# One decode step of attention with a small dense layer: per-head results transposed on TensorE, finished on VectorE and mixed one piece apart, with the last values in four pieces

## The chip, the cores and the metric

The kernel runs on one core of one Trainium2 chip. The metric is the device time of one execution in microseconds (us); the number given for a kernel is the median of its runs. The profile comes from one separate execution, in which the hardware profiler records every instruction and every DMA packet.

## What is computed

The step takes two tokens (batch 2, one position each, width 448), a layer norm of them, and adds three things: the tokens themselves, attention over the last 4096 keys of a cache of 32768, and a dense layer with a mish activation (1792 wide). Cut to what matters:

```python
xn = _layernorm(x)
q  = (xn @ wq)                      # 16 heads of 256, 2 per key/value head
k, v = the last 4096 keys and values of each of the 8 key/value heads
p  = softmax(q k^T * 256**-0.5)
o  = p @ v
out = x + o.reshape(B, 1, 4096) @ wo + (mish(xn @ w1 + b1) @ w2)
```

Everything is bfloat16 in memory, and sums are kept in fp32. The bulk of the data is the cache: for each of 8 key/value heads 4 MiB of keys and 4 MiB of values, in all 64 MiB; the weights bring the total that is read to 77.67 MB.

## The kernel before

The 4096 keys of both batches are laid over 128 partitions, 64 keys in each (`T = 64`), and cut into four pieces of 16 (`TH`, `NH`). The main loop (`for i in range(Hkv + 1)`, L589 on) has one turn for each key/value head `i`, and an inner loop over its four pieces, numbered `s = 4 i + piece`.

For each piece:

- `turn(s+1)` (L404): VectorE transposes the next piece of keys in 32x32 blocks, `kt<-k`.
- `scores(s)` (L416): eight matmuls on TensorE, `sc<-kt,qdiag`, then two exponentials on ScalarE (L430), which also sum.
- `turn_p(s-1)` (L442): VectorE transposes the exponentials of the piece before, `pT<-p`. After the last piece of a head it forms the sums (L449, L451).

For each head, one head later:

- `values(i-1)` (L477): 32 matmuls `o<-v,pT`, with 8 rows of output: two positions at once (`NP = 2`), times batch and head. Only where the position in the row and the half of the output belong together is the result of use. The denominator is one fp32 matmul (L458, two records) and a reciprocal `rec` on VectorE (L462). ScalarE copies the output to SBUF, `o_sb` (L486).
- `values_fixed` (L554): the form that the last two heads (6 and 7, `NFIX = 2`) use instead: 128 matmuls with the values as the stationary operand, so that the result comes out already transposed; `scale_o` (L498) then divides.

Two heads later, after piece 0 of head `i`, `close(i-2)` runs `finish` and `mix`:

- `finish` (L516, L526, L532, L539), heads 0 to 5 only: TensorE multiplies `o_sb` by columns of an identity, 8 calls in fp32, which sum the two positions in PSUM as they transpose; then VectorE multiplies by `rec`, multiplies by `own` (which head a partition belongs to) and adds the two heads, giving `oTm`.
- `mix` (L220, for the last head L237): four matmuls of width 448 by `wo`, accumulated in one PSUM bank `psE`. For head 7 the output is split over four column groups (`psA`), into which `carry` (L249, L237) has brought the sum so far.

At the end `psA` is cast to `res` (L627) and written out (L628).

Transfers: all large loads are issued by SP in program order, keys of head i+1, then values of head i, then `wo` of head i (L373, L390, L398). A load waits for its buffer: keys and values have two buffers each. The keys of head 7 come in two pieces, its values in three (cut at 32, 56 and 64 of the 64 positions), its `wo` in two.

The order on each engine is the order in which the program is written: `issue_in_order` ties every instruction to the one before it on its engine. So where `finish` stands in the program decides which instructions of VectorE and TensorE it is queued behind and which wait behind it.

Of the kernel before, what the change touches and what calls it, by code (L numbers as in the profile page):

```python
# [34 lines left out]
def kernel(  # L35
# [13 lines left out]
    nc = tc.nc  # L49
# [48 lines left out]

    x_bf = consts.tile([Bsz, D], BF16)
    nc.scalar.dma_start(out=x_bf[:, :], in_=A_x.flatten_outer_dims())  # L100
    b1_sb = consts.tile([1, F], BF16)
    nc.scalar.dma_start(out=b1_sb[:, :], in_=B_b1.rearrange("(o f) -> o f", o=1))


    def v_tile():
# [97 lines left out]
    for par in range(2):  # L203
        for x in range(NX):
# [5 lines left out]
                scalar2=None,  # L210
                op0=ALU.mult,
            )
    ones = consts.tile([1, Bsz], BF16)
    nc.vector.memset(ones[:], 1.0)


    psE = ps_a.tile([Bsz, D], FP32, name="psE")

# [77 lines left out]
                )  # L296


    act_bf = consts.tile([P, NF, NX, Bsz], BF16)
    dense = {}  # L300

# [13 lines left out]

    def dense_in():
        w1_v = dense.pop("w1").rearrange("p s (q c) -> p s c q", c=NF)
        b1_v = b1_sb[:].rearrange("o (x q c) -> o x c q", x=NX, c=NF)
        hT_ps = ps_m.tile([P, NF, NX, Bsz], FP32, tag="m", name="hT_ps")
        for c in range(NF):  # L320
            for s in range(NS):
                nc.tensor.matmul(
                    hT_ps[:, c, :, :].rearrange("p x b -> p (x b)"),
                    lhsT=w1_v[:, s, c, :],
                    rhs=xs[:, s, :, :].rearrange("p x b -> p (x b)"),
                    start=(s == 0),
                    stop=False,
                    skip_group_check=True,
                )
            for x in range(NX):  # L330
                nc.tensor.matmul(
                    hT_ps[:, c, x, :],
                    lhsT=b1_v[:, x, c, :],
                    rhs=ones[:, :],
                    start=False,
                    stop=True,
                    skip_group_check=True,
                )
        shape = [P, NF, NX, Bsz]
        h_sb = consts.tile(shape, FP32, name="h_sb")  # L340
        nc.vector.tensor_copy(out=h_sb[:], in_=hT_ps[:])
        u_sb = consts.tile(shape, FP32, name="u_sb")
        nc.scalar.activation(out=u_sb[:], in_=h_sb[:], func=ACT.Exp)
        t_sb = consts.tile(shape, FP32, name="t_sb")
        nc.vector.scalar_tensor_tensor(
            out=t_sb[:], in0=u_sb[:], scalar=2.0, in1=u_sb[:], op0=ALU.add, op1=ALU.mult
        )
        den = consts.tile(shape, FP32, name="den_sb")
        nc.vector.tensor_scalar(
            out=den[:], in0=t_sb[:], scalar1=2.0, scalar2=None, op0=ALU.add  # L350
        )
        nc.vector.reciprocal(out=den[:], in_=den[:])
        nc.vector.tensor_tensor(out=t_sb[:], in0=t_sb[:], in1=den[:], op=ALU.mult)
        nc.vector.tensor_tensor(out=act_bf[:], in0=h_sb[:], in1=t_sb[:], op=ALU.mult)  # L354
# [24 lines left out]
    def load_v(i, cuts=(0, T)):  # L379
        t = v_tile()  # L380
        load_cache(t, A_v_cache, i, cuts)
        v_t[i] = t[:].rearrange("p (t d) -> p t d", t=T)
# [17 lines left out]
    def turn(s):  # L400
        kt = kt_pool.tile([P, TH * Dh], BF16, tag="kt", name="kt")
        i, half = divmod(s, NH)
        k = k_t[i] if half < NH - 1 else k_t.pop(i)
        nc.vector.transpose(  # L404
            out=kt[:].bitcast(FP32),
            in_=k[:, half * TH * Dh : (half + 1) * TH * Dh].bitcast(FP32),
        )
        kt_t[s] = kt
# [47 lines left out]
    def denominator(i):  # L456
        den = ps_m.tile([P, BR], FP32, tag="m", name="den")
        nc.tensor.matmul(  # L458
            den[:], lhsT=ones_f[:], rhs=state.pop(("sums", i))[:], start=True, stop=True
        )  # L460
        rec = small.tile([P, BR], FP32, tag="rec", name="rec")
        nc.vector.reciprocal(out=rec[:], in_=den[:])  # L462
        return rec
# [6 lines left out]
    def values(i):  # L470

        po = ps_o.tile([NR, NP * Dh], FP32, tag="o", name="o")
        v = v_t.pop(i)
        state["rec", i] = denominator(i)
        for u in range(T // NP):
            piece, uh = divmod(u, TH // NP)
            nc.tensor.matmul(  # L477
                po[:],
                lhsT=pT_t[i * NH + piece][:, uh * NP * Q : (uh + 1) * NP * Q : HS],
                rhs=v[:, u * NP : (u + 1) * NP, :].rearrange("p t d -> p (t d)"),  # L480
                start=(u == 0),
                stop=(u == T // NP - 1),
            )
        o_sb = small.tile([NR, NP, NJ, rep, PH], FP32, tag="o_sb", name="o_sb", bufs=1)
        for u in range(NP):
            nc.scalar.copy(  # L486
                out=o_sb[:, u, :, :, :],
                in_=po[:, u * Dh : (u + 1) * Dh]
                .rearrange("r (m j) -> r j m", j=NJ)
                .unsqueeze(2)  # L490
                .to_broadcast([NR, NJ, rep, PH]),
            )
        state["o", i] = o_sb
# [12 lines left out]
        )  # L506
        state["oT", i] = oT

    def finish(i):

        o_sb = state.pop(("o", i))
        pq = ps_q.tile([P, NJ * BR], FP32, tag="q", name="q")
        pqv = pq[:].rearrange("p (j r) -> p j r", j=NJ)
        for j in range(NJ):
            for u in range(NP):
                nc.tensor.matmul(  # L516
                    pqv[:, j, :],
                    lhsT=o_sb[:, u, j, :, :].rearrange("r h m -> r (h m)"),
                    rhs=ident_f[0:NR, u * BR : (u + 1) * BR],
                    start=(u == 0 and j == 0),  # L520
                    stop=(u == NP - 1),
                    skip_group_check=True,
                )
        rec = state.pop(("rec", i))
        o = small.tile([P, NJ, Bsz, rep], FP32, tag="osum", name="osum")
        nc.vector.tensor_tensor(  # L526
            out=o[:].rearrange("p j b h -> p j (b h)"),
            in0=pqv,
            in1=rec[:].unsqueeze(1).to_broadcast([P, NJ, BR]),
            op=ALU.mult,  # L530
        )
        nc.vector.tensor_tensor(  # L532
            out=o[:].rearrange("p j b h -> p j (b h)"),
            in0=o[:].rearrange("p j b h -> p j (b h)"),
            in1=own[:].rearrange("p b h -> p (b h)").unsqueeze(1).to_broadcast([P, NJ, BR]),
            op=ALU.mult,
        )
        oT = small.tile([P, NJ, Bsz], BF16, tag="oTm", name="oTm")
        nc.vector.tensor_tensor(  # L539
            out=oT[:], in0=o[:, :, :, 0], in1=o[:, :, :, 1], op=ALU.add  # L540
        )
        state["oT", i] = oT

    def values_fixed(i):
# [19 lines left out]
    def mix(kvh):  # L564
        oT = state.pop(("oT", kvh))
        w = wo_t.pop(kvh)
        put = add_last if kvh == Hkv - 1 else add
        if kvh < Hkv - NFIX:
            for j in range(NJ):
                add(oT[:, j, :], w[:].rearrange("p h (c d) -> p (h c) d", c=ND)[:, j, :])  # L570
            return
        for h in range(rep):
            for c in range(ND):
                put(
                    oT[:, c, h, :],
                    w[:, h, c * D : (c + 1) * D],
                    stop=(kvh >= Hkv - 2 and h == rep - 1 and c == ND - 1),
                )

    def close(i):  # L580
        if i < Hkv - NFIX:
            finish(i)
        mix(i)

    load_k(0)
    load_dense()
    project()
# [3 lines left out]
    for i in range(Hkv + 1):  # L591
        if i + 1 < Hkv:
            load_k(i + 1, (0, T) if i + 1 < Hkv - 1 else (0, T // 2, T))
        if i < Hkv:
            load_v(i, (0, T) if i < Hkv - 1 else (0, T // 2, 7 * T // 8, T))
            load_wo(i, parts=1 if i < Hkv - 1 else 2)
            for piece in range(NH):
                s = i * NH + piece
                if s + 1 < NSTEP:
                    turn(s + 1)  # L600
                scores(s)
                if s >= 1:
                    turn_p(s - 1)
                if s == NSTEP - 1:
                    turn_p(s)
                if piece == 0 and i > 1:
                    close(i - 2)
            if i + 2 < Hkv:
                build_q(i + 2)
        else:  # L610
            close(i - 2)
            carry()
        if i == 0:
            dense_in()
            dense_out()
        if i >= 1:
            if i - 1 < Hkv - NFIX:
                values(i - 1)
            else:
                values_fixed(i - 1)  # L620
        if i == Hkv:
            close(i - 1)

    res = consts.tile([Bsz, D], BF16)
    for n in range(NO):
# [34 lines left out]
```

The softmax here doesn't subtract the row's maximum and nothing guards it: scores larger than these inputs give would overflow.

## Time and profile before

| what | value |
|---|---|
| median of 11 runs | 192.11 us (190.89 to 193.04) |
| the profiled execution's own time | 191.89 us |
| its span, first to last instruction | 190.0 us |
| TensorE busy, share of the span | 154.3 us, 81% |
| VectorE busy | 108.7 us, 57% |
| ScalarE busy | 45.4 us, 24% |
| GpSimd busy | 16.4 us, 9% |
| moved by DMA | 77.81 MB, mean 409 GB/s over the span |
| granted TensorE clock, mean | 0.898 of full |

In the profile a group reads "line, engine, operation, out<-in, shape, count, busy time, mean of one". Fp32 matmuls leave two records for each call. "PEld" is the load of the stationary operand, which runs beside the matmuls. A wait is put down to the instruction that ended it. The chain of work is followed back from the last instruction, at each step to what released it.

### The profile page before, as it was taken

To read this page: it belongs to the slowest core of one execution; us is meant where nothing else is said; L and a number is where in the kernel's file an instruction comes from. 1 tells how busy PE (TensorE), PEld (TensorE's weight loads), DVE (VectorE), ACT (ScalarE), POOL (GpSimd) and SP (SyncE) were. 2 spreads that over 40 slices of the span, in tenths; PEclk is the share of its full clock that TensorE was granted. 3 is DMA by queue.
4 is the path that set the end of the run, shared out by engine and by line. 5 is a ranking of instruction groups with operands and counts; after the bars stand their busy time and mean duration, and the time that the engine had idled before them with its cause. 6 is when DMAs were issued, how large, how long until landed. Compare 5 with 4: busy or idle time off the path is not lost.

```text
span 190.0 us, 2498 instructions
## 1 busy us (share of the span) xinstructions
PE 154.3 (81%) x981; PEld 75.0 (39%) x981; DVE 108.7 (57%) x144; ACT 45.4 (24%) x148; POOL 16.4 (9%) x74
## 2 busy tenths in 40 slices
PE   0397099905989989998999889779895889989983
PEld 0133033902334344435343534253442534534762
DVE  6703697059572957097806990399209957576211
ACT  3003115200152223222332242222403151404201
POOL 7000600300003000300030003000300000000000
PEclk9999759955899978999699999999999999979755
DMA  6999999999999999999999899999999999999950
GB/s 218 429 458 434 394 480 415 407 438 421 441 434 435 443 424 441 422 441 419 450 424 436 382 473 434 407 441 424 434 441 441 396 439 448 438 406 421 417 224 0
DMA packets 4884, 77.81 MB, mean 409 GB/s; under 512 B 517, under 2 KB 1033, under 8 KB 2186
## 3 DMA queue, kind: packets, MB, share of 16 engines
q1 hardware_dynamic: 4868, 77.66, 95.8%
q8 instruction: 7, 0.11, 0.2%
q14 instruction: 3, 0.02, 0.0%
q10 hardware_dynamic: 6, 0.01, 0.0%
HBM read 77.67 MB, written 0.00 MB: 409 GB/s over the span
## 4 chain that ended last, share of the span: by engine, by line
DMA 49%; PE 31%; DVE 16%; SPq 1%; issue 1%; ACT 1%; ACTq 0%; DVEq 0%
DMA k<-in_A_k_cache_dram 49%; DVE kt L404 12%; PE sc L416 10%; PE o L477 7%; PE psE L220 4%; PE q L516 4%; PE q L554 4%; DVE pT L442 2%; PE psA L237 1%; ACT p L430 1%; PE den L458 0%; SPq L114 0%; DVE osum L532 0%; DVE osum L526 0%; DVE oTm L539 0%
## 5 line engine op out<-in xcount | busy, mean ns | idle before, releaser
L404 DVE STREAM_TRANSPOSE kt<-k 128x2048 f32<-128x2048 f32 x32 | 73.1, 2288 | 45.8 <-DMA k<-in_A_k_cache_dram 45.8
L416 PE MATMUL sc<-kt,qdiag 128*128 128x512 bf16 x256 | 65.0, 407 | 13.4 <-DVE kt L404 13.4
L430 ACT ACTIVATE p<-sc,off 128x256 bf16<-128x256 f32 x64 | 33.1, 544 | 71.5 <-PE sc L416 70.8
L416 PEld LDWEIGHTS <-qdiag 128*128 128x128 bf16 x256 | 24.6, 101 | 53.6 <-issue 18.6
L477 PE MATMUL o<-v,pT 128*8 128x512 bf16 x192 | 42.5, 379 | 0.0
L477 PEld LDWEIGHTS <-pT 128*8 128x8 bf16 x192 | 17.2, 92 | 22.4
L442 DVE STREAM_TRANSPOSE pT<-p 128x512 bf16<-128x512 bf16 x32 | 21.7, 678 | 6.4 <-ACT p L430 6.4
L289 POOL COPY qdiag<-qt 32x16 bf16<-32x16 bf16 x64 | 12.9, 248 | 120.5 <-PE sc L416 102.9
L486 ACT COPY o_sb<-o 8x512 f32<-8x512 f32 x12 | 6.3, 573 | 36.3 <-PE o L477 36.3
L516 PEld LDWEIGHTS q<-ident_f,o_sb 8*128 8x128 f32 x96 | 11.1, 186 | 2.5 <-issue 2.5
L430 ACT ACTIVATION_READ_ACCUMULATOR p<-sc,off 128x1 f32 x64 | 11.7, 183 | 0.0
L516 PE MATMUL q<-ident_f,o_sb 8*128 8x4 f32 x96 | 11.7, 249 | 0.0
L269 PE MATMUL q_ps<-v,xq 128*128 128x512 bf16 x28 | 9.1, 504 | 2.1 <-DVE xq L260 2.1
L220 PE MATMUL psE<-v,act_bf 128*2 128x448 bf16 x14 | 4.8, 528 | 6.4 <-DVE act_bf L354 6.4
L220 PE MATMUL psE<-wo,oTm 128*2 128x448 bf16 x24 | 6.4, 394 | 4.1 <-DVE oTm L539 4.1
L554 PEld LDWEIGHTS <-v 128*128 128x128 bf16 x256 | 7.3, 102 | 0.0
L554 PE MATMUL q<-pT,v 128*128 128x4 bf16 x256 | 7.1, 168 | 0.0
L269 PEld LDWEIGHTS <-xq 128*128 128x128 bf16 x28 | 3.4, 124 | 7.8 <-issue 3.8
L279 DVE CAST q_sb<-q_ps 128x512 bf16<-128x512 f32 x2 | 1.3, 686 | 8.6 <-PE q_ps L269 8.6
L220 PEld LDWEIGHTS <-act_bf 128*2 128x2 bf16 x14 | 1.5, 116 | 9.3 <-DVE act_bf L354 6.5
L190 PE MATMUL xnT_ps<-ident,xn_bf 2*128 2x2 bf16 x7 | 0.5, 166 | 5.7 <-DVE xn_bf L138 5.7
L526 DVE TENSOR_TENSOR osum<-q,rec 128x16 f32<-128x16 f32 x6 | 1.0, 174 | 6.7 <-PE q L516 6.7
(62 smaller groups left out, 49.0 us busy)
## 6 DMA issues: line engine op xcount, KB each, us to landing
k<-in_A_k_cache_dram SPq DMA_DIRECT2D x7, 4096.0 KB, 28.4
v<-in_A_v_cache_dram SPq DMA_DIRECT2D x7, 4096.0 KB, 27.6
k<-in_A_k_cache_dram SPq DMA_DIRECT2D x2, 2048.0 KB, 24.3
v<-in_B_w_dram SPq DMA_DIRECT2D x2, 1568.0 KB, 24.8
wo<-in_A_wo_dram SPq DMA_DIRECT2D x7, 448.0 KB, 28.6
v<-in_A_wq_dram SPq DMA_DIRECT2D x1, 2048.0 KB, 7.7
v<-in_A_v_cache_dram SPq DMA_DIRECT2D x1, 2048.0 KB, 15.0
v<-in_A_wq_dram SPq DMA_DIRECT2D x1, 1536.0 KB, 10.9
```

Of the source, the lines that this page charges most:

```text
L220: nc.tensor.matmul(psE[:], lhsT=lhsT, rhs=w, start=start, stop=stop, skip_group_check=True)
L237: nc.tensor.matmul(part(n), lhsT=lhsT, rhs=w[:, n * DO : (n + 1) * DO], start=start, stop=stop, tile_position=(0, n * Q), skip_group_check ...
L269: nc.tensor.matmul(ps[u][:], lhsT=xq[:, s, :, :].rearrange("p j k -> p (j k)"), rhs=wq_sb[:, s, u * N5 : (u + 1) * N5], start=(s == 0), st ...
L289: nc.gpsimd.tensor_copy(out=tv[rows, :, e, j * Q : (j + 1) * Q : HS].rearrange("p n (b h) -> p n b h", b=Bsz), in_=qv[rows, :, h0 : h0 + r ...
L404: nc.vector.transpose(out=kt[:].bitcast(FP32), in_=k[:, half * TH * Dh : (half + 1) * TH * Dh].bitcast(FP32),)
L416: nc.tensor.matmul(psc[:], lhsT=qdiag[i % NW][:, n * NE + e, :], rhs=ktv[:, n, e, :, :], start=(n == 0 and e == 0), stop=(n == NB - 1 and ...
L430: nc.scalar.activation(out=pv[:, b, :, :], in_=sv[:, b, :, :], func=ACT.Exp, scale=scale, bias=off[:, b : b + 1], accum_out=state["rs", i] ...
L442: nc.vector.transpose(out=pT[:], in_=p_t.pop(s)[:])
L477: nc.tensor.matmul(po[:], lhsT=pT_t[i * NH + piece][:, uh * NP * Q : (uh + 1) * NP * Q : HS], rhs=v[:, u * NP : (u + 1) * NP, :].rearrange ...
L486: nc.scalar.copy(out=o_sb[:, u, :, :, :], in_=po[:, u * Dh : (u + 1) * Dh] .rearrange("r (m j) -> r j m", j=NJ) .unsqueeze(2) .to_broadcas ...
L516: nc.tensor.matmul(pqv[:, j, :], lhsT=o_sb[:, u, j, :, :].rearrange("r h m -> r (h m)"), rhs=ident_f[0:NR, u * BR : (u + 1) * BR], start=( ...
L554: nc.tensor.matmul(po[:, c, :], lhsT=vv[:, t, c, :], rhs=pTv[:, th, 0:Q:HS], start=(t == 0 and c == 0), stop=(t == T - 1), skip_group_chec ...
```

## The change

- `finish` is split. `turn_o(i-2)` does the TensorE part where `close` stood, after piece 0; `finish(i-2)` does the VectorE part in piece 1, after that piece's `turn` and ahead of its `scores`; `mix(i-2)` comes at the end of piece 1. In the program's order TensorE now has scores, transpositions, scores, mix; and VectorE has one more `kt` transposition ahead of the finishing instructions.
- The eight fp32 matmuls of `finish` become eight fp32 transpositions with an 8-column identity each. They no longer sum the two positions; all 8 rows come out.
- VectorE then multiplies the two useful halves (two instructions of 128x16) and sums positions and heads with one reduction. The mask `own` is multiplied into `rec` once, in `values`, by one instruction of 128x4 (`recm`).
- The values of head 7 come in four pieces (cut at 32, 52, 60 and 64) in place of three.
- The bias of the dense layer is laid over two partitions and added by one matmul in place of two for each of seven groups (`half` in place of `ones`).

```diff
-    b1_sb = consts.tile([1, F], BF16)
-    nc.scalar.dma_start(out=b1_sb[:, :], in_=B_b1.rearrange("(o f) -> o f", o=1))
+    b1_sb = consts.tile([NX, HF], BF16)
+    nc.scalar.dma_start(out=b1_sb[:, :], in_=B_b1.rearrange("(x f) -> x f", x=NX))
...
-            for x in range(NX):
-                nc.tensor.matmul(
-                    hT_ps[:, c, x, :],
-                    lhsT=b1_v[:, x, c, :],
-                    rhs=ones[:, :],
...
+            nc.tensor.matmul(
+                hT_ps[:, c, :, :].rearrange("p x b -> p (x b)"),
+                lhsT=b1_v[:, c, :],
+                rhs=half[:].rearrange("o x b -> o (x b)"),
...
-        state["rec", i] = denominator(i)
+        rec = denominator(i)
+        state["rec", i] = small.tile([P, BR], FP32, tag="recm", name="recm")
+        nc.vector.tensor_tensor(
+            out=state["rec", i][:],
+            in0=rec[:],
+            in1=own[:].rearrange("p b h -> p (b h)"),
+            op=ALU.mult,
+        )
...
-    def finish(i):
+    def turn_o(i):
 
         o_sb = state.pop(("o", i))
-        pq = ps_q.tile([P, NJ * BR], FP32, tag="q", name="q")
-        pqv = pq[:].rearrange("p (j r) -> p j r", j=NJ)
+        pq = ps_q.tile([P, NJ * NP * NR], FP32, tag="q", name="q")
+        pqv = pq[:].rearrange("p (j u r) -> p j u r", j=NJ, u=NP)
         for j in range(NJ):
             for u in range(NP):
-                nc.tensor.matmul(
-                    pqv[:, j, :],
-                    lhsT=o_sb[:, u, j, :, :].rearrange("r h m -> r (h m)"),
-                    rhs=ident_f[0:NR, u * BR : (u + 1) * BR],
-                    start=(u == 0 and j == 0),
-                    stop=(u == NP - 1),
-                    skip_group_check=True,
+                nc.tensor.transpose(
+                    pqv[:, j, u, :],
+                    o_sb[:, u, j, :, :].rearrange("r h m -> r (h m)"),
+                    ident_f[0:NR, 0:NR],
                 )
+        state["pq", i] = pqv
+
+    def finish(i):
+        pqv = state.pop(("pq", i))
         rec = state.pop(("rec", i))
-        o = small.tile([P, NJ, Bsz, rep], FP32, tag="osum", name="osum")
...
+        o = small.tile([P, NJ, NP, BR], FP32, tag="osum", name="osum")
+        for u in range(NP):
+            nc.vector.tensor_tensor(
+                out=o[:, :, u, :],
+                in0=pqv[:, :, u, u * BR : (u + 1) * BR],
+                in1=rec[:].unsqueeze(1).to_broadcast([P, NJ, BR]),
+                op=ALU.mult,
+            )
         oT = small.tile([P, NJ, Bsz], BF16, tag="oTm", name="oTm")
-        nc.vector.tensor_tensor(
-            out=oT[:], in0=o[:, :, :, 0], in1=o[:, :, :, 1], op=ALU.add
-        )
+            nc.vector.tensor_reduce(
+                out=oT[:],
+                in_=o[:].rearrange("p j u (b h) -> p j b u h", b=Bsz),
+                axis=AXIS.XY,
+                op=ALU.add,
+            )
...
-            load_v(i, (0, T) if i < Hkv - 1 else (0, T // 2, 7 * T // 8, T))
+            load_v(i, (0, T) if i < Hkv - 1 else (0, T // 2, 13 * T // 16, 15 * T // 16, T))
...
                 if s + 1 < NSTEP:
                     turn(s + 1)
+                if piece == 1 and i > 1:
+                    finish(i - 2)
                 scores(s)
...
                 if piece == 0 and i > 1:
-                    close(i - 2)
+                    turn_o(i - 2)
+                if piece == 1 and i > 1:
+                    mix(i - 2)
             if i + 2 < Hkv:
                 build_q(i + 2)
         else:
-            close(i - 2)
+            mix(i - 2)
             carry()
...
         if i == Hkv:
-            close(i - 1)
+            mix(i - 1)
```

## Prediction

> **What bounds the kernel now.** I read the slices of the page first, then the DMA issues, then the chain of work over the last 35 us, and last the granted clock there.
>
> ```profile
> PEclk9999759955899978999699999999999999979755
> DMA  6999999999999999999999899999999999999950
> ...
> v<-in_A_v_cache_dram SPq DMA_DIRECT2D x7, 4096.0 KB, 27.6
> ...
> v<-in_A_v_cache_dram SPq DMA_DIRECT2D x1, 1536.0 KB, 18.1
> v<-in_A_v_cache_dram SPq DMA_DIRECT2D x1, 512.0 KB, 18.7
> wo<-in_A_wo_dram SPq DMA_DIRECT2D x2, 224.0 KB, 18.6
> ```
>
> The DMA engines are full from the first slices to slice 38 of 40. A 4 MiB load takes 27.6 us from issue to landing though its bytes alone need 4.19 MB / 0.43 MB per us = 9.8 us: some 18 us of older loads stand ahead of each at its issue. A buffer released a few microseconds later costs nothing, so before about 180 us an engine can neither gain nor lose time for the kernel. The last loads are issued at about 164.1, 164.7 and 166.0 us; with the landing times above, the values of head 7 are complete at 183.4 and the last half of `wo` at 184.6. The end of the span is 190.0, 5.4 us later. What lies in between is shown by the chain:
>
> ```profile
> 156.45 7.01 PE o L477 x32
> 163.46 1.85 PE sc L416 x8
> 165.30 1.89 PE q L516 x16
> ...
> 167.63 0.18 DVE oTm L539
> 167.81 0.04 issue
> 167.85 1.27 PE psE L220 x4
> 169.12 6.61 PE sc L416 x24
> 175.73 0.12 PE den L458 x2
> 175.85 3.43 PE q L554 x128
> ...
> 182.95 3.43 PE q L554 x128
> 186.38 0.02 issue
> 186.40 0.18 DVE oT L498
> 186.58 0.04 issue
> 186.62 0.65 PE psA L237 x16
> ```
>
> TensorE works without a DMA wait from 156.45 on and is late: when the last values land at 183.4 it has just begun the 128 matmuls of head 7 (end 186.37). So the end is set by TensorE's backlog, and the floor under it is the last load. In the backlog are the fp32 matmuls L516 (1.9 us) and a wait for `oTm` (167.17 to 167.85, 0.68 us).
>
> ```profile
> 167.00:168.00 1.00, 0.33 (x3) 0.17 (x3) 0.72 (x4) 0.00 (x0) 0.00 (x0) 1.00 0.91 393
> 168.00:169.00 1.00, 1.00 (x4) 0.17 (x2) 1.00 (x1) 0.00 (x0) 0.00 (x0) 0.64 1.14 492
> 169.00:170.00 1.00, 1.00 (x4) 0.39 (x4) 1.00 (x2) 0.00 (x0) 0.00 (x0) 0.50 1.14 492
> 171.00:172.00 1.00, 1.00 (x4) 0.39 (x3) 1.00 (x1) 0.00 (x0) 0.00 (x0) 0.65 0.81 321
> ```
>
> The third number from the end is the granted clock. Right after L516 and that wait it falls to half, from 168.3 to 171.65 us, and this slows the scores: 24 matmuls in 6.61 us, while 16 of the turn before took 3.66 (0.229 each, 5.5 for 24).
>
> [...] No run here shows an fp32 transposition yet. [...]
>
> **The change part by part**, on the profiled execution (own time 191.89, of which 190.0 span; 0.22 under the median 192.11).
>
> 1. Transpositions for matmuls. Now 16 records, 1.94 us for a head. Eight transpositions of one pass each at 0.112 are 8 x 0.112 + 0.14 (drain) = 1.04, a gain of 0.9. [...] I take 0.9. It counts once, at head 5's results (165.23); the other five groups lie under the DMA stream.
>
> 2. `finish` and `mix` a piece later. At the tail TensorE goes from the transpositions (end 166.3) straight to scores of piece 29, whose keys are turned at 163.2. VectorE turns piece 30 meanwhile (from 164.1 to 166.4; its keys landed earlier: 9.3 MB follow them in the stream, 184.2 - 9.3 / 0.43 = 162.6), finishes from 166.4 to 167.0, and `mix` on TensorE at about 168.1 finds `oTm` ready. The wait of 0.68 us goes. Next late is VectorE: `pT` (0.67) and piece 31 (2.3) end at 170.0; TensorE needs piece 31 at about 171, so nothing new waits.
>
> 3. In turns 2 to 6 of the loop VectorE starts from a late landing of keys, and there the same order adds a wait. In turn 6: piece 26 is turned at 148.5 to 150.8, `finish` follows to 151.5, and `mix` stands in TensorE's queue from about 149.6 (scores of 25 end) to 151.6. Queued behind are the scores of 26 (then 152.5 to 154.3). The scores of 27 need piece 27, turned at 152.0 to 154.3 as now: VectorE loses nothing, since its 0.20 us wait for L516 goes and `recm` comes. They begin at 154.4 as now (154.43). [...]
>
> 4. The half clock at 168.3. The low-activity stretch that called it (165.23 to 167.85, 2.6 us) shrinks to 1.0 us of transpositions. If the spell goes, its cost goes: 3.35 us at half speed, 1.65 us. Bounds 0 and 1.65.
>
> 5. VectorE: two products of 0.175 and one reduction (nearest row L539, 0.17; L449 on fewer outputs 0.12) for three instructions of 0.17; plus `recm` 6 x 0.17 after `rec`. At head 5 it stands ahead of piece 29 and moves its end from 163.18 to 163.35, which TensorE wants at 166.3: nothing.
>
> 6. Values in four pieces. SP issues one DMA more, 0.54 to 0.6 us, before `wo` of head 7; that is issued at 166.6 in place of 166.0, with 18 us of stream ahead: nothing. The last piece is 4 positions in place of 8: 8 matmuls after its landing in place of 16, at 0.028 us (3.55 / 128) a gain of 0.22, but only if TensorE is there first. Bounds 0 and 0.22, and up to 0.2 lost if smaller pieces slow the stream.
>
> 7. Bias: seven matmuls less at 34 to 38 us, about 0.13 each, where TensorE then idles 6.4 us for `act_bf`; `half` delays `xq` by 0.1 us at 8.5 us, under a stream 18 us ahead: nothing.
>
> Sum on the path. Points 1 and 2: 0.9 + 0.68 = 1.58. L554 of head 7 then ends at 186.37 - 1.58 = 184.8, just after the last load (184.6): span 188.4. With point 4 too, TensorE would be 3.2 us earlier, but the loads stop it: values 183.4, 8 matmuls and drain to 183.8, `oT` to 184.05, the second half of `mix` not before 184.6, ended at 185.0 in place of 187.2: gain 2.2, span 187.8. The phase of the clock is free, so I take 2.0: 191.89 - 2.0 = 189.9, and from the median 192.11 - 2.0 = 190.1 us.
>
> **The rivals.** A, the forecast: backlog gone, the end a little behind the last load; 190.1, by itself 189.4 to 191.0. B: an fp32 transposition is as slow as the matmul pair, and half clock comes all the same; only the wait goes, 192.11 - 0.7 = 191.4. [...] C: the stream ends later (five small loads at its end, or a slower transfer), which takes back the gain: 192.1. Against it: the same bytes behind the same backlog. [...]
>
> **How the numbers follow.** A 0.72, B 0.14, C 0.07, D 0.07. The likeliest is A. Some of A's upper end falls to "same". 0.5% is 0.96 us, about what a measurement of this kernel can tell from no change: faster 0.72, same 0.20, slower 0.08. The range runs from 189.2 (all of 2.2, a fast transposition, a stream at its best) to 191.7, which takes in B.
>
> **What would show it.** The transposition group at half the records and about 1 us for a head; no wait of TensorE for `oTm` at the tail, but one of about 2 us in each of turns 2 to 6; full clock from 165 to 175; L477 of head 5 ending at 163.5 still; the last DMA at 184 to 185; `psA` starting near 184.5 to 185. I am wrong if the L477 end moves, if the stream ends later, or if the records of the transpositions stay at sixteen.

## The result, and the profile after

The changed kernel takes 189.81 us (median of 12 runs, 189.50 to 190.28), the kernel before 191.79 us (median of 47 runs, 190.87 to 193.08). The ratio is 0.989, with a 95% interval from 0.987 to 0.992. The profiled execution took 189.74 us, its span 187.9 against 190.0. The runs of the changed kernel also lie closer together: 0.8 us from the lowest of 12 to the highest, against 2.2 us in 47. A ratio here and below compares runs within 1.5% of the fastest of their kernel; only the kernel with the repeated transpositions has longer ones, six of 22.

The slices of the page after, granted clock and DMA:

```profile
PEclk9999558955699999995799999985999999999855
DMA  6999899999999999999999999999999999999990
```

The stream is as it was, and full one slice further towards the end of a shorter span. The mean granted clock of the profiled execution is lower than before (0.870 against 0.898): there is more half clock in the middle (84.5 to 91.35 and 125.45 to 132.3 us), and it is gone from where it counted. The chain of waits of the changed kernel, from 155 us on (start, duration, what):

```profile
155.84 0.12 PE den L458 x2
155.96 7.02 PE o L484 x32
...
166.22 0.59 SPq L398
166.81 0.04 issue
166.85 17.76 DMA wo<-in_A_wo_dram
184.62 0.04 issue
184.66 0.46 PE psA L234 x8
185.12 0.23 ACT res L634
```

Before, TensorE and VectorE stood in every line of this chain from 156 us to the end of the last `mix`, but for gaps of 0.02 to 0.04 us. Now a transfer ends it: the second half of `wo` for head 7 lands at 184.62, eight matmuls follow, and the end. The landing itself has hardly moved (184.6 before). The time came out of the 2.7 us between that landing and the end of the last `mix`, of which 0.5 are left.

Where TensorE's lateness went is seen in the order of time, changed kernel, TensorE's own lines (start, duration, engine, line, operation; in brackets its idle time and what ended it):

```profile
162.90 1.91 PE L416 MATMUL sc<-kt,qdiag 128*128 128x512 bf16 x8
164.74 0.66 PE L523 MATMUL q<-ident_f,o_sb 8*128 8x8 f32 x8
165.33 1.91 PE L416 MATMUL sc<-kt,qdiag 128*128 128x512 bf16 x8
167.18 0.92 PE L217 MATMUL psE<-wo,oTm 128*2 128x448 bf16 x4
168.03 3.66 PE L416 MATMUL sc<-kt,qdiag 128*128 128x512 bf16 x16
172.32 3.56 PE L562 MATMUL q<-pT,v 128*128 128x4 bf16 x128 [0.52 <-DMA v<-in_A_v_cache_dram]
181.75 2.22 PE L562 MATMUL q<-pT,v 128*128 128x4 bf16 x64 [0.94 <-DMA v<-in_A_v_cache_dram]
```

The transpositions are eight records in 0.66 us where sixteen in 1.94 stood. `mix` starts with no wait for `oTm`. The last 16 score matmuls need 3.66 us, at full clock. From 172 us on TensorE waits for values twice, 0.52 and 0.94 us, and the last 64 matmuls take 2.22 us where the 64 before them took 1.85, so some 0.35 us more of waiting lie between their pieces: it is ahead of the loads. The granted clock (third number from the end), changed kernel, in the microseconds in which it was halved before:

```profile
167.00:168.00 1.00, 1.00 (x6) 0.25 (x4) 1.00 (x2) 0.72 (x3) 0.00 (x0) 1.00 0.76 328
168.00:169.00 1.00, 1.00 (x6) 0.49 (x6) 1.00 (x1) 0.36 (x2) 0.00 (x0) 1.00 1.06 459
169.00:170.00 1.00, 1.00 (x6) 0.39 (x5) 1.00 (x2) 0.02 (x1) 0.00 (x0) 1.00 1.14 492
171.00:172.00 1.00, 0.80 (x6) 0.47 (x3) 0.71 (x1) 0.34 (x3) 0.00 (x0) 1.00 0.84 333
```

### The profile page after: what moved, and what is told of

Same layout as the page of the kernel before. It is cut to its first block, busy times and chain, and to the rows that moved or that the text cites. A ratio compares the mean times of both kernels' runs of the same rounds, so it can differ in the third digit from the quotient of the medians.

```text
span 187.9 us, 2389 instructions
## 1 busy us (share of the span) xinstructions
PE 148.8 (79%) x926; PEld 67.4 (36%) x926; DVE 108.6 (58%) x150; ACT 45.3 (24%) x148; POOL 16.3 (9%) x74
## 4 chain that ended last, share of the span: by engine, by line
DMA 66%; DVE 20%; PE 8%; SPq 2%; ACT 1%; issue 1%; ACTq 0%; DVEq 0%
DMA k<-in_A_k_cache_dram 57%; DVE kt L404 16%; DMA wo<-in_A_wo_dram 9%; PE sc L416 4%; PE o L484 4%; DVE pT L442 3%; SPq L373 2%; ACT p L430 1%; PE psE L217 0%; SPq L114 0%; DVE sums L451 0%; SPq L398 0%; DVE oTm L544 0%; DVE recm L476 0%; PE psA L234 0%
## 5 line engine op out<-in xcount | busy, mean ns | idle before, releaser
L416 PE MATMUL sc<-kt,qdiag 128*128 128x512 bf16 x256 | 66.9, 413 | 16.2 <-DVE kt L404 15.9
L484 PE MATMUL o<-v,pT 128*8 128x512 bf16 x192 | 42.5, 379 | 0.0
L484 PEld LDWEIGHTS <-pT 128*8 128x8 bf16 x192 | 17.2, 92 | 22.4
L217 PE MATMUL psE<-v,act_bf 128*2 128x448 bf16 x14 | 5.4, 574 | 6.4 <-DVE act_bf L354 6.4
L266 PE MATMUL q_ps<-v,xq 128*128 128x512 bf16 x28 | 8.2, 465 | 2.1 <-DVE xq L257 2.1
L562 PE MATMUL q<-pT,v 128*128 128x4 bf16 x256 | 7.6, 169 | 1.5 <-DMA v<-in_A_v_cache_dram 1.5
L523 PEld LDWEIGHTS q<-ident_f,o_sb 8*128 8x128 f32 x48 | 4.1, 162 | 3.4 <-issue 3.4
L217 PEld LDWEIGHTS <-oTm 128*2 128x2 bf16 x24 | 1.7, 89 | 8.5 <-DVE oTm L544 6.2
L523 PE MATMUL q<-ident_f,o_sb 8*128 8x8 f32 x48 | 4.7, 220 | 0.0
```

Of the source, the lines that this page charges most:

```text
L217: nc.tensor.matmul(psE[:], lhsT=lhsT, rhs=w, start=start, stop=stop, skip_group_check=True)
L266: nc.tensor.matmul(ps[u][:], lhsT=xq[:, s, :, :].rearrange("p j k -> p (j k)"), rhs=wq_sb[:, s, u * N5 : (u + 1) * N5], start=(s == 0), st ...
L416: nc.tensor.matmul(psc[:], lhsT=qdiag[i % NW][:, n * NE + e, :], rhs=ktv[:, n, e, :, :], start=(n == 0 and e == 0), stop=(n == NB - 1 and ...
L484: nc.tensor.matmul(po[:], lhsT=pT_t[i * NH + piece][:, uh * NP * Q : (uh + 1) * NP * Q : HS], rhs=v[:, u * NP : (u + 1) * NP, :].rearrange ...
L523: nc.tensor.transpose(pqv[:, j, u, :], o_sb[:, u, j, :, :].rearrange("r h m -> r (h m)"), ident_f[0:NR, 0:NR],)
L562: nc.tensor.matmul(po[:, c, :], lhsT=vv[:, t, c, :], rhs=pTv[:, th, 0:Q:HS], start=(t == 0 and c == 0), stop=(t == T - 1), skip_group_chec ...
```

## The experiments

The theory (A): TensorE's backlog set the end, partly made of work and a wait, partly of a half-clock spell; the change removes more than it has to, and the last load is the new limit. The rivals: the transpositions alone carry it, the later place alone carries it, the smaller last piece carries it, or the clock plays no part. Each kernel was timed beside runs of the kernel before on the same chip, whose medians were 192.18 (first four), 191.87 (next four) and 192.21 us (last four). The changed kernel was not timed again beside them; differences from it are taken from its 189.81, which one version in each group that was expected to take the same time comes close to (189.58, 189.84 and 189.74).

### One part at a time

**Only the later place.** The kernel before, with the three calls set where the changed kernel has them; the fp32 matmuls and VectorE's instructions stay.

```diff
-    def finish(i):
+    def turn_o(i):
...
+        state["pq", i] = pqv
+
+    def finish(i):
+        pqv = state.pop(("pq", i))
         rec = state.pop(("rec", i))
...
+                if piece == 1 and i > 1:
+                    finish(i - 2)
                 scores(s)
...
-                    close(i - 2)
+                    turn_o(i - 2)
+                if piece == 1 and i > 1:
+                    mix(i - 2)
```

> The kernel before with only the order changed: the fp32 matmuls of finish stay, the finishing on VectorE and mix come one piece later. Theory A (the end was set by TensorE's backlog, the floor is the last load): at the tail the wait of 0.68 us for oTm goes and nothing else, unless the half-clock spell goes too; 191.1 with the spell, 189.8 without, so between 189.8 and 191.1 by its phase. Rival T (the cheaper transpositions carry the gain): 191.8, as before. Rival D (a slower middle): over 192.5, with the values of head 5 ending later than 163.5.

Measured: 189.79 us, ratio 0.990 (0.988 to 0.993). This is the whole gain, at the favourable end of what A allowed, although the sixteen records of L516 are still there. Its chain of waits:

```profile
156.12 7.02 PE o L477 x32
163.15 0.02 issue
163.16 0.54 SPq L373
163.71 0.05 issue
163.76 18.45 DMA v<-in_A_v_cache_dram
182.21 0.05 issue
182.25 1.88 PE q L558 x64
184.13 0.02 issue
184.16 0.18 DVE oT L498
```

Here, too, a load bounds the end: the middle one of the three loads of values (1536 KB) lands at 182.21, and the 64 matmuls that are left run through behind it. The clock is full from 48.2 to 177.9 us. Rival T falls.

**Only the transpositions.** The changed kernel with the old order and three pieces, so with VectorE's new instructions too. The new bias stays: by the author's account the old one, laid out on one partition, does not fit in SBUF beside the larger tiles of the sums; no run shows it.

```diff
-                if piece == 1 and i > 1:
-                    finish(i - 2)
...
                     turn_o(i - 2)
-                if piece == 1 and i > 1:
+                    finish(i - 2)
                     mix(i - 2)
...
-            load_v(i, (0, T) if i < Hkv - 1 else (0, T // 2, 13 * T // 16, 15 * T // 16, T))
+            load_v(i, (0, T) if i < Hkv - 1 else (0, T // 2, 7 * T // 8, T))
```

> The kernel before with only the fp32 transpositions, the sums on VectorE and the new bias, all in the old place after piece 0 (the old bias does not fit beside the larger tiles); values of head 7 in three pieces. Theory A: the 16 records of 1.94 us become 8 of 0.66, so TensorE is 1.28 us less late, the wait for oTm stays near 0.7, and the low-activity stretch is 1.3 us instead of 2.6, so the half clock should mostly go: 189.8 to 190.5. Rival M (the later place carries the gain): 191.8.

Measured: 189.97 us, ratio 0.991 (0.989 to 0.994). The wait for `oTm` at the tail is still there:

```profile
PE psE L217 <- DVE oTm L544: 0.6, 1, 0.6
```

The clock is full from 48.4 to 178.1 us. Rival M falls as well: either part alone is enough.

**Only the pieces and the bias.**

```diff
-            load_v(i, (0, T) if i < Hkv - 1 else (0, T // 2, 7 * T // 8, T))
+            load_v(i, (0, T) if i < Hkv - 1 else (0, T // 2, 13 * T // 16, 15 * T // 16, T))
```

(and the bias of two partitions, as in the change).

> The kernel before with only the four pieces of the last values and the bias in one matmul per group. Theory A: TensorE is behind the last load anyway, so nothing: 191.8. Rival P (the smaller last piece is what shortens the end): 190 or below. A third reading, that one more small load makes the stream longer: 192.0 or above.

Measured: 191.71 us, ratio 0.999 (0.997 to 1.001): nothing. Its chain ends as that of the kernel before does, to within 0.05 us (head 7's last matmuls end at 186.37), and half clock stands at 168.6 to 172.0 again.

**The change without the four pieces** (the same line, the other way round).

> The changed kernel with the last values in three pieces as before. Theory A: with TensorE ahead of the loads, 16 matmuls follow the last piece in place of 8, which is 0.22 us, but the last half of wo lands about 1 us after the values and hides it: 189.8. Rival P (the pieces matter once TensorE is ahead): 190.0 or more, and the second half of mix starts without a wait for wo.

Measured: 189.58 us, ratio 0.989 (0.987 to 0.992). With TensorE ahead, too, the fourth piece is worth nothing that can be seen: the matmuls of the values then end at 184.04, while `wo` lands about as late. One part of A's reason did not hold, that `wo` lands 1 us later and hides the 16 matmuls: `mix` ran through behind the values, and the profile names no wait for `wo`. The two are level, and the end is in the same place.

### The clock

**More work in the kernel before.** Where it idled just before the half clock, it does eight score matmuls a second time, with no reader.

```diff
     def close(i):
         if i < Hkv - NFIX:
             finish(i)
+        if i == Hkv - NFIX - 1:
+            filler((i + 2) * NH + 1)
         mix(i)
```

> The kernel before with more work: in the last turn that has a finish, the eight score matmuls of piece 29 are also done once more, between the fp32 matmuls and mix, into a tile that nobody reads. That is 1.73 us of busy TensorE, of which 0.68 lie where it waits for oTm anyway: 1.05 us more on the path. Clock theory (the low-activity stretch of the fp32 matmuls and the wait calls half clock at 168.3, which costs 1.65 us): the stretch is filled, full clock from 165 to 175, and the time goes down by some 0.6 us, 191.2, with 190.5 to 191.5 as its range. Rival (only the amount of work counts): 192.8 or above.

Measured: 191.47 us, ratio 0.998 (0.996 to 1.000). The kernel does about 1 us more on TensorE's path and takes 0.4 us less by the medians. The interval touches 1, so it is not slower, and "faster" is at the edge; the 192.8 of the rival is out. Two lines of its windows and its chain of waits show the cause:

```profile
168.00:169.00 1.00, 1.00 (x6) 0.33 (x5) 1.00 (x1) 0.00 (x0) 0.00 (x0) 1.00 1.21 524
170.00:171.00 1.00, 1.00 (x6) 0.48 (x5) 1.00 (x2) 0.00 (x0) 0.00 (x0) 1.00 0.67 279
```

```profile
165.27 1.87 PE q L516 x16
167.14 1.85 PE sc_more L585 x8
168.99 0.85 PE psE L220 x4
169.84 5.34 PE sc L416 x24
```

The 24 score matmuls take 5.34 us at full clock; they took 6.61 in the kernel before. `psE` takes 0.85 in place of 1.27. So 1.7 us of lost clock came back for 1.1 us of work. That the half clock merely fell elsewhere in this execution can be ruled out: the two earlier spells stand where they stood (69.4 to 72.8 and 89.9 to 93.3 us here, 69.3 to 72.7 and 89.8 to 93.2 before), and only the one behind the filled gap is missing.

**More tiny work in the changed kernel.** The eight transpositions of head 5 are done seven times.

```diff
-        for j in range(NJ):
+        for j in list(range(NJ)) * (7 if i == Hkv - NFIX - 1 else 1):
             for u in range(NP):
                 nc.tensor.transpose(
```

> The changed kernel with the eight transpositions of head 5 repeated six times more: 48 x 0.066 = 3.2 us more of TensorE work of low activity at the place where the fp32 matmuls stood. Nearly as much work as in the run with the score matmuls of two pieces twice. Clock theory: a stretch of 3.8 us of tiny instructions calls half clock for the scores after it, 1.65 us on top: 192.7 to 193.1. Rival (only the amount counts): 191.2 to 191.6.

Measured: 192.64 us, median of 22 runs that spread from 190.23 to 194.76; 192.53 without the six longest, and a ratio of 1.000 (0.998 to 1.003). That is just under the 192.7 to 193.1 of the clock theory, and 0.9 over the top of what the rival allowed. It is also 1.0 us more than the kernel below that adds 3.46 us of full-width work, for less added work (3.2 us at full clock). The profiled run (194.26) is one of the six. In it half clock lasts from 167.5 to 174.35, 6.85 us or twice the 3.35 of the kernel before, and begins inside the string: 39 of the 56 transpositions start in the 2.4 us before 167.5, the other 17 take 2.0 us, some 4.3 us in all. So 3.7 us were added there, of which some 0.5 us is half clock itself. The wide spread of the runs would fit a spell that varies in length and place, but no second run was profiled.

### How far TensorE is ahead

**Eight, then sixteen score matmuls more at the tail.**

```diff
-        for n in range(NB):
+        for n in list(range(NB)) * (2 if s in (NSTEP - 2,) else 1):
             for e in range(NE):
                 nc.tensor.matmul(
                     psc[:],
```

and `(NSTEP - 2, NSTEP - 1)` for sixteen.

> The changed kernel with the eight score matmuls of piece 30 done twice: 1.73 us more of busy TensorE at the tail. Theory A (TensorE is ahead of the loads; its waits for values are 0.52 and 0.94 us there): the reserve of about 1.5 us takes nearly all of it, 189.8 to 190.2. Rival (TensorE still sets the end): 191.5.

Measured: 189.84 us, ratio 0.988 (0.983 to 0.992): 1.73 us of work cost nothing.

> The changed kernel with the score matmuls of pieces 30 and 31 done twice: 3.46 us more. Theory A: beyond the reserve of about 1.5 us every microsecond counts, so 1.6 to 2.0 us more than the changed kernel, 191.4 to 191.8. If the reserve is larger than read: 190.5 or below. If TensorE sets the end all along: 193.2.

Measured: 191.52 us, ratio 0.997 (0.995 to 1.000): the second 1.73 us cost 1.68. So the reserve is 3.46 - 1.71 = 1.75 us by the medians. The two waits in the profile had shown 1.46; with the 0.35 us of waiting inside the last 64 matmuls it is 1.8. Beyond it TensorE sets the end again, and the spread of the runs comes back with it (190.73 to 192.72).

The profiled run of each of these two kernels was its longest (190.87 and 192.72), and each shows a half-clock spell of 6.8 and 6.9 us in the middle (146.2 to 153.0 and 145.7 to 152.6). These are windows of the first; up to there its program is that of the changed kernel:

```profile
146.00:147.00 1.00, 1.00 (x4) 0.20 (x2) 1.00 (x1) 0.00 (x0) 0.00 (x0) 0.59 1.06 459
148.00:149.00 1.00, 1.00 (x5) 0.41 (x5) 0.96 (x4) 0.34 (x2) 0.00 (x0) 0.50 0.91 393
150.00:151.00 1.00, 1.00 (x3) 0.29 (x2) 1.00 (x3) 0.00 (x0) 0.00 (x0) 0.50 0.97 404
152.00:153.00 1.00, 1.00 (x4) 0.21 (x2) 1.00 (x1) 0.81 (x4) 0.00 (x0) 0.50 1.06 451
```

Rival D was the slower middle: a half-clock spell here in turn 6, called by the wait of `mix` that the prediction puts at 149.6 to 151.6. The place fits, the route does not, for both spells begin before that wait, soon after TensorE has waited 2.0 to 2.3 us, until 144.8, for turned keys. The kernel before has such a wait, too (2.02 us, to 144.88), and full clock after it; what decides is not shown. The values of head 5 (L484) then end at 163.92 and 163.86 in place of 162.98, so 6.8 or 6.9 us of half clock cost some 0.9 us. The changed kernel has 1.75 to spare; with eight matmuls more the reserve is spent, and the 190.87 stands 1.0 us over the median.

### The last load

**0.459 MB less behind the last keys**, in the changed kernel and in the kernel before.

```diff
     def load_wo(kvh, parts=1):
+        if kvh == Hkv - NFIX:
+            wo_t[kvh] = wo_t[kvh - 1]
+            return
```

> The changed kernel without the load of wo for head 6, whose mix uses the tile of head 5 instead; this leaves out 0.459 MB of the stream, and it lies behind the last keys, so only the loads after it come earlier, by 0.459 / 0.43 = 1.07 us. Theory A (the last load sets the end, with TensorE some 1.5 us ahead): 188.7 to 188.9. Rival (TensorE or something else sets the end): 189.8.

Measured: 188.72 us, ratio 0.983 (0.978 to 0.987), so 1.09 us under the changed kernel. In its chain of waits TensorE is just level again: the matmuls of head 7 run through without a wait and `mix` follows at once.

```profile
179.69 3.43 PE q L565 x128
...
183.15 0.18 DVE oT L508
...
183.37 0.65 PE psA L234 x10
```

> The kernel before without the load of wo for head 6 (its mix uses the tile of head 5). The same 1.07 us leave the stream behind the last keys. Theory A (TensorE's backlog sets the end of the kernel before): no change, 191.6 to 192.1. Rival (the stream sets it): 190.8.

Measured: 191.78 us, ratio 0.997 (0.995 to 0.999) against the 192.21 of the kernel before beside it. The same bytes that are worth 1.09 us after the change are worth some 0.4 before it (0.1 to 0.9 by the interval), where A said none and the rival 1.07; whether that is more than a difference in where the half clock fell in these runs was not settled. In its trace the values of head 7 are in 1 us earlier (the piece of 1536 KB 17.1 us after its issue, 18.1 before), and the chain of waits does not move:

```profile
182.92 3.43 PE q L557 x128
...
186.59 0.65 PE psA L237 x14
```

**The order of the last loads.** The changed kernel with `wo` of head 7 issued ahead of its values.

```diff
+            if i == Hkv - 1:
+                load_wo(i, parts=2)
             load_v(i, (0, T) if i < Hkv - 1 else (0, T // 2, 13 * T // 16, 15 * T // 16, T))
-            load_wo(i, parts=1 if i < Hkv - 1 else 2)
+            if i < Hkv - 1:
+                load_wo(i, parts=1)
```

> The changed kernel with wo of head 7 issued ahead of its values, so that the last bytes of the stream are values in place of wo; the same bytes. Theory A (what counts is the last landing and the work behind it): behind the last values stand 8 matmuls and drain 0.4, oT 0.25 and 16 matmuls of mix 0.6, in place of 8 matmuls of mix 0.46 behind the last wo: 0.7 to 0.8 more, 190.5. Rival (the order of the last loads is free): 189.8.

Measured: 190.59 us, ratio 0.993 (0.989 to 0.996), 0.78 over the changed kernel. Its chain of waits has the values piece by piece:

```profile
182.83 1.23 PE q L562 x40
184.06 0.01 issue
184.07 0.59 PE q L562 x16
184.66 0.00 issue
184.66 0.39 PE q L562 x8
185.06 0.02 issue
185.08 0.18 DVE oT L505
185.26 0.04 issue
185.30 0.65 PE psA L234 x10
```

The last values are in by 184.66, where the last `wo` had been in at 184.62; what stands behind them is longer, as computed.

### The wait in the middle

**`mix` after piece 2**, so that the scores of piece 2 no longer stand behind its wait.

```diff
-                if piece == 1 and i > 1:
+                if piece == 2 and i > 1:
                     mix(i - 2)
```

> The changed kernel with mix after piece 2 instead of piece 1, so that in turns 2 to 6 TensorE no longer stands 1.5 to 2 us in front of it before the scores of piece 2. Theory A (that wait is covered by the transposition of the last piece of keys): no change, 189.6 to 190.0. Rival (the wait costs): 189.3 or less is not possible under the last load, so the rival would show as less spread only; a time over 190.5 would mean that mix now meets something later.

Measured: 189.74 us, ratio 0.987 (0.983 to 0.991): the same time. But TensorE does not get the wait back. In turn 6 the scores of piece 2 now wait themselves, for VectorE, which turns their keys until about 150.6 in either order; those of piece 3 wait 0.42 us for theirs.

```profile
150.87 1.90 PE L416 MATMUL sc<-kt,qdiag 128*128 128x512 bf16 x8 [1.30 <-DVE osum L536]
152.70 0.92 PE L217 MATMUL psE<-wo,oTm 128*2 128x448 bf16 x4
154.04 1.90 PE L416 MATMUL sc<-kt,qdiag 128*128 128x512 bf16 x8 [0.42 <-DVE kt L404]
```

The values of head 5 then end at 163.07, against 162.98. So the wait that the change puts into the middle costs nothing, because the transposition of keys takes up that time anyway. No version here is measurably faster than the changed kernel, except the one that leaves out a load.

## Why the prediction was right

**The time.** 190.1 us was forecast and 189.81 measured. The forecast gain was 2.0 us, the measured one 1.98 by the medians and 2.15 by the profiled executions; the 0.29 us between forecast and result is that the kernel before has a median of 191.79 over more runs, not 192.11. That the gain was met to 0.02 us is luck: 2.0 was chosen between two sums, 1.6 and 2.2, and the median of the kernel before lies between 191.79 and 192.21 from one set of runs to the next. That the gain is capped near 2.2 by the loads was reasoned, and holds.

**The floor.** The last load was put at 184.6 and the span at 187.8 with the clock spell gone: it lands at 184.62, span 187.9. That the end was TensorE's before and the stream's now is shown from both sides: bytes taken from the stream's end count in full after the change, and for less than half before it, where the chain of waits does not follow them. One sentence on the way there does not hold as it stands. That before about 180 us an engine can neither gain nor lose time for the kernel is contradicted by the forecast's own sum and by the runs: what TensorE saved between 165 and 171 us is the gain. For the middle of the kernel the last experiment agrees with it. The 0.43 MB per us of the sums is the mean of the 37 full slices of the page before, 430 GB/s; 25 of them stand at 420 to 450, the others reach from 382 to 480.

**Point 1, transpositions.** 1.04 us for a head was taken, 0.66 measured: eight records, their starts 0.066 us apart where the matmul records stood 0.112 apart. That a transposition is one pass of 0.112 us, the pace of a record of the fp32 matmul, was the author's estimate, and no run shows it; the gain is 1.28, not 0.9.

**Point 2, the wait.** The 0.68 us went, and VectorE was not late: `oTm` was ready at 166.62, `mix` started at 167.18.

**Point 3, turns 2 to 6.** A wait of 2 us in front of `mix` was expected; in turn 6 it is 1.56 us:

```profile
PE psE L217 <- DVE oTm L544: 1.6, 1, 1.6
```

Over the whole run the row of the matmuls gives 3.1 us in two such waits, the row of their weight loads 6.2 us in five, less than the 2 us in each of five turns that were forecast. The end of L484 came at 162.98, not at 163.46. The prediction had named a move of this end as a sign of being wrong. It feared a later end, and got an earlier one, which its account of turn 6 has no term for. The keys of head 6 landed 0.3 us earlier in this execution, and the finishing on VectorE is shorter, 0.44 us (150.54 to 150.98) where 0.59 had stood (148.69 to 149.28). From the start of VectorE on these keys to the end of L484 it is 20.85 us here and was 21.03 before.

**Point 4, the clock.** Full clock from 132.3 to 176.65 us. The prediction took the spell as a gain that depends on a free phase of the clock and is capped by the loads. The cap is how it came out, and with the quiet stretch filled the spell is gone. That the phase is free, on which the 2.0 was chosen, was the author's assumption, and no run shows it; what they show is that the spell at the tail stands in all three profiles of kernels with the old order and the old matmuls and no fill, and in none of those with either part of the change, but for the one with the repeated transpositions. A second spell the sum put at nothing: at the very end the clock is half, from 178.5 us before and from 176.65 after. It slows the `mix` of head 6, which takes 1.65 us before, 1.18 after, and 0.92 in the two kernels with one part each, where it comes ahead of that spell.

**Points 5 to 7.** `recm` takes 0.16 us and is hidden; four pieces and the bias, put into the kernel before, are worth nothing (ratio 0.999), and the pieces are worth nothing in the changed kernel either. But what the bias is for the prediction did not see: by the author's later account it makes room in SBUF for the larger tiles.

**What the sum did not say.** It added points 1 and 2 to come just to the last load. The runs show that either alone comes there: in the profile of each the spell is gone, and with its 1.65 us and 0.68 or 1.28 us more TensorE is ahead of the loads, which it waits for 0.93 and 0.79 us. All together, 1.28 + 0.68 + 1.65 = 3.6 us were taken from TensorE, some 2.1 of them could be used, and the rest is the reserve of 1.5 to 1.75 us. The reserve is also a likely reason for the smaller spread: where TensorE sets the end (before, the pieces alone, the fill, the kernel before without a load, sixteen matmuls more), runs differ by 1.2 to 2.8 us, and where a load sets it, mostly by 0.2 to 0.8. But the first are 22 to 59 runs of a kernel and the second 4 to 12, which by itself makes their spread smaller.

**What stays open.** The runs of the kernel with the pieces alone fall into groups (spans of about 189.1, 189.9 and 190.8 us), and so do those of the kernel before. Only runs of the middle group were profiled. The lowest are hardly runs without the spell at the tail: by the sums above such a run would span 190.0 - 1.65 = 188.4 us, and of the 22 runs of the one and 116 of the other none is under 188.9. Why one low-activity stretch calls half clock and another does not was not settled: in the profile of the kernel before three of the six groups of fp32 matmuls are followed by a spell, and two of the three, at 69 and 90 us, stand in the three other profiles with these matmuls in the old place as well.

## What to carry to other kernels

Read the end of a stream-bound kernel as a race between the last landing and the engine that must use it: which of the two ends last decides whether a microsecond of either counts, and leaving out a small load behind the last input, in both kernels, tells it in one run of each (here 1.09 us after the change and some 0.4 before). Here a string of tiny matmuls and a wait (1.94 and 0.68 us) cost TensorE not only their own length but half speed for 3.35 us after them. Shortening them got rid of both (2 us, up to the limit of the loads); filling the wait with useless full-width work got back the clock alone, 1.7 us for 1.1 us of work, and by the medians no more than 0.4. Once the transfer was last, further savings on the engine only bought reserve, 1.5 to 1.75 us here.

## What the runs showed that was not expected

Here an fp32 transposition of 8 x 128 (8 moving columns) left one record where an fp32 matmul with the same stationary shape and 4 moving columns left two (8 and 16 records for a head), and a string of them started every 0.066 us at full clock, against 0.225 us for a two-record matmul; at half clock (from 85.60 us) a group of eight takes 1.02 us in place of 0.66. The 128 bf16 matmuls of `values_fixed` with 4 moving columns did not feel the clock: they take 3.56 us at full clock (head 6 in the changed kernel, from 172.32) and 3.56 at half (head 7 in the kernel before, from 182.81), while the `mix` ahead of the latter takes 1.65 us in place of 0.92. Two products of 128x16 from PSUM on VectorE overlap in the changed kernel: the pair took 0.22 us with records of 0.13 to 0.16 each, where one took 0.17 before. In the kernel with eight score matmuls more a half-clock spell lasted 6.8 us (146.2 to 153.0) and cost only 0.94 us at the end of the values: TensorE's work in it grew by some 3 us, but two waits of 0.50 and 1.56 us, which the changed kernel has there, were taken up.
